# One written order for three schedulers: attention's end, token mixing and the MLP's first rounds of a fused layer

## The chip, the core and the metric

The kernel runs on one core of a Trainium2 chip. The metric is the device time of one execution in microseconds (us). The engines are called here as the profile calls them: PE (matrix products; PEld is its weight load), DVE (vector), ACT (scalar), POOL (GpSimd) and SP, which here only issues transfers. Each engine works through its own queue in order, and a wait at the head of a queue holds everything behind it.

## What is computed

The reference chains three blocks over x of shape 2 x 768 x 512 (two batches, 768 tokens, 512 channels):

```python
mask = q_bucket[:, :, :, None] == k_bucket[:, :, None, :]          # 6 hash bits for each token
scores = np.where(mask, 1 / np.sqrt(D) * q @ k.T, -1e9)            # 2 batches x 8 heads, 768 x 768, D = 64
x = softmax(scores) @ v                                            # heads side by side: 2 x 768 x 512
theta = x @ w_theta
y = w_tok_r @ (x * np.cos(theta)) + w_tok_i @ (x * np.sin(theta))  # mixes tokens: 768 x 768, for each batch
u = x + y
x = u + np.maximum(u @ w_ch, 0)
xn = (x - mean) / np.sqrt(var + 1e-6) * g_ln
out = x + np.maximum(xn @ w_ch1, 0) @ w_ch2                        # 512 -> 2048 -> 512
```

## The kernel before

Products run with 32-bit operands that are each split into a high and a low part; three products (high x high, high x low, low x high) stand for one. So nearly every operand costs an ACT copy that makes the high part and a subtraction that makes the low part, on DVE or on POOL. Weights arrive as 64-bit numbers and are rebuilt as 32-bit ones first: `conv_y` (ACT), `conv_s` (POOL, the `cs` tiles), `conv_bits` (two DVE instructions), then the high and the low part.

The work has four stages.

- **Attention**, 48 blocks of 256 query rows. One step of the loop touches several blocks at once: scores `s`, row maximum `m`, exponential `p`, normalised `pn` on POOL, three groups of four 128x128 transposes on PE (`U0` to `U2`, tile `t`), the high part on ACT (`H0` to `H2`, `pth`), the low part on DVE (`L0` to `L2`, `ptl`), the product with v (`PV`, tile `o`), and its eviction in two parts (`O` on ACT, `X` on DVE) into `XT`. The order of these steps is written by hand (`plan_s`, `plan`, `plan_b`) up to step 47. The last steps, which only finish blocks 45 to 47, were in the scheduler's hands.
- **Mixing.** For each batch b and each of six blocks j of 128 tokens, `mix_z` splits a block of x (`xh`, `xl`), transposes it on PE (`xps` or `xth`), copies that into `U` on ACT, makes 12 products of 512 columns with w_theta (tile `th` or `xth`), reduces the angle (DVE `t`, POOL `kk`, DVE `r`, DVE clamp of `r`), takes Abs and two Sin on ACT, multiplies by x on DVE, and splits both results (tile `z` or `arena`: high part ACT, low part DVE). These feed the token product `acc`: two halves of the output tokens, six blocks j, three groups t of 128 output tokens, two batches, six products of 512 columns each. The first half of the output was in the scheduler's order; the second half (`half1`) is an order written by hand in which one step (`mix.N`) holds both batches, 12 products. `mix_add` on DVE adds `acc` into `U`.
- **Channel product** with w_ch (12 chunks `ch_*`: transposes `ut`, split `uxh`/`uxl`, 12 products, DVE residual and statistics), layer normalisation (`ln_*`, `xn`), its transposes and sums (`xb_*`); these stand between the mixing steps and the MLP's first rounds, in the orders `half1` and `trans`.
- **MLP**, 16 rounds (`prod`, `snap`, `h_*`, `o_mm`, `o_add`). Rounds 0 to 2 stand in `trans`, the fourth and later ones in the repeated orders `odd` and `even`.

PSUM has few banks: in the mixing, the transposed block and the angle of one b share a bank (tags `T1`, `T2`), or two halves of one tile (`S0`, `S1`) for the first blocks.

Of the kernel before, what the change touches and what calls it, by code (L numbers as in the profile page):

```python
# [29 lines left out]
PI_LO = 3.1415925  # L30
# [3 lines left out]
def attn_moe_kernel(  # L34
# [80 lines left out]
    def conv_s(t, y, s):  # L115
        pool.tensor_scalar(out=s, in0=f(t)[:, :, 1], scalar1=0.0, scalar2=1.0, op0=ALU.mult, op1=ALU.mult)  # L116
# [553 lines left out]
    steps += [(k, plan_b if k - 2 in bq else plan) for k in range(4, NPER + last)]  # L670
    for k, now in steps:
        if k == NPER:
            order.close()
            bctx.close()
# [19 lines left out]

    up = ctx.enter_context(tc.tile_pool(name="u", bufs=1, reuse_waits="tile"))
# [7 lines left out]
    tok_t, tok_st = {}, {}  # L703

    def tok_load(half, j):
        tok_st[half, j] = [
            w_load(mp, w[j * 128:(j + 1) * 128, half * TW:(half + 1) * TW], bufs=4) for w in (wrT, wiT)
        ]

    def tok_conv(half, j):  # L710
        th, tl = (mp.tile([128, 2, TW], F32R, tag=x, bufs=2, name=f"{x}{half}{j}") for x in ("tokh", "tokl"))
        for x, t in enumerate(tok_st.pop((half, j))):
            w_conv(mp, t, th[:, x, :], tl[:, x, :])
        tok_t[half, j] = (th, tl)

    def ch_conv():
        WA["h"], WA["l"] = (
            const.tile([128, 4, 512], F32R, tag=f"X{x}", name=f"ch{x}") for x in range(2)
        )
        for c in range(4):  # L720
            for x in range(2):
                r = slice(256 * x, 256 * x + 256)
                w_conv(
                    mp, w_load(mp, w_ch[c * 128:(c + 1) * 128, r], "cst", 4), WA["h"][:, c, r], WA["l"][:, c, r], vec
                )

    def mix_banks(b, j):

        if j == 0:
            t = psum.tile([128, 2, 512], F32, tag=f"S{b}", name=f"xth{b}")  # L730
            return lambda x: t[:, x, :]
        return lambda x: bank(f"T{1 + b}", ("xps", "th")[x] + f"{b}{j}")

    z_s = {}
# [4 lines left out]
    def mix_z(b, j):  # L739
        c = b * NI + j  # L740
        if j == 0:
            z = mp.tile([128, 2, 2, 512], F32R, tag=f"z{b}0", name=f"z{b}0")
        else:
            z = arena[0][:, 2 * j - 2 + b, :].rearrange("p (y h n) -> p y h n", y=2, h=2)
        src = XT[b][:, :, j * 128:(j + 1) * 128]
        xh, xl = (up.tile([128, 512], F32R, tag=x, bufs=2, name=f"{x}{c}") for x in ("xh", "xl"))
        xh, xl = (x.rearrange("p (a s) -> p a s", a=4) for x in (xh, xl))
        cast(act, xh, src)
        sub(vec, xl, src, xh)
        banks = mix_banks(b, j)  # L750
        xps = banks(0)
        x = U[:, c, :]
        for d in range(4):
            pe.transpose(xps[:, d * 128:(d + 1) * 128], src[:, d, :], ident)
        act.activation(x, xps, AF.Copy)
        ps = banks(1)
        k = 0
        for d in range(4):
            for lt, w in ((xh, "h"), (xh, "l"), (xl, "h")):
                pe.matmul(ps, lt[:, d, :], WA[w][:, d, :], start=(k == 0), stop=(k == 11))  # L760
                k += 1
        t, kk, r = (tmp(y) for y in ("t", "kk", "r"))
# [12 lines left out]
        z_s[b, j] = z
# [3 lines left out]
    def mix_acc(half):  # L779
        for b in range(B):  # L780
            t = psum.tile([128, 2, 512], F32, tag=f"S{b}", name=f"acc{half}{b}")
            acc_t[half, b, 0], acc_t[half, b, 1] = t[:, 0, :], t[:, 1, :]
            acc_t[half, b, 2] = bank("T0" if b == 0 else "O", f"acc{half}{b}")

    def mix_mm(half, j, t):
        if j == 0 and t == 0:
            mix_acc(half)
        th, tl = tok_t[half, j]
        for b in range(B):
                acc, z = acc_t[half, b, t], z_s[b, j]  # L790
                k = 0
                for x in range(2):
# [7 lines left out]
    def mix_add(t, half=1):  # L800
        for b in range(B):
            u = U[:, b * NI + half * TH + t, :]
            vec.tensor_tensor(out=u, in0=acc_t[half, b, t], in1=u, op=ALU.add)
# [513 lines left out]
```

## Time and profile before

| | |
|---|---|
| median of three runs | 691.59 us (691.1 to 694.54) |
| the profiled execution's own time | 691.84 us |
| its span in the trace | 690.0 us, 11241 instructions |
| PE busy | 668.8 us, 97% of the span |
| DVE / ACT / POOL busy | 553.0 / 418.6 / 358.3 us |

The 1.84 us between span and time lie around the traced span. "Busy" of PE counts each product from its start to a modelled end, and products overlap, so an idle stretch of PE in the trace is a little shorter than the time that it costs.

### The profile page before, as it was taken

The page shows a single profiled execution, that of the slowest core. Times are in us where ns is not written, and L with a number is a line of the kernel's source. Part 1 is how long each engine was busy: PE and PEld are TensorE (multiplying, and loading weights), DVE is VectorE, ACT ScalarE, POOL GpSimd, SP SyncE. Part 2 cuts the span into 40 slices and gives each one's busy share as a digit, 9 for nine tenths or more (in the row PEclk, how much of TensorE's full clock was granted, in tenths as well). Part 3 has the DMA queues.
Part 4 walks back from the last instruction along what each step waited for, and adds up shares of the span by engine and source line. Part 5 has one row for each costly group of instructions (what it writes and reads, how often), then busy time and mean ns, then how long its engine had stood idle before and what let it go on. Part 6 is the DMA issues. An engine that isn't in the chain of part 4 may idle for free.

```text
span 690.0 us, 11241 instructions
## 1 busy us (share of the span) xinstructions
PE 668.8 (97%) x3790; PEld 593.1 (86%) x3790; DVE 553.0 (80%) x958; ACT 418.6 (61%) x864; POOL 358.3 (52%) x500
## 2 busy tenths in 40 slices
PE   9999999999999899999799989999999999999997
PEld 8899999999999777878578868889889898998986
DVE  5899988999999998897996376986666776767654
ACT  6799998999999866576442544463334434344321
POOL 5788998776776823334365975251523325050500
PEclk9999999999999999999999999999999999999999
DMA  8875654575550411112341301101121111111013
GB/s 250 208 156 154 156 113 110 126 161 126 136 153 18 138 46 47 47 46 62 129 119 58 123 1 61 62 1 34 62 90 62 61 62 62 61 62 62 0 47 137
DMA packets 32229, 62.23 MB, mean 90 GB/s; under 512 B 4466, under 2 KB 11460, under 8 KB 32173
## 3 DMA queue, kind: packets, MB, share of 16 engines
q1 hardware_dynamic: 32173, 61.53, 31.2%
q8 instruction: 30, 0.49, 0.3%
q14 instruction: 26, 0.21, 0.1%
HBM read 39.98 MB, written 3.15 MB: 62 GB/s over the span
## 4 chain that ended last, share of the span: by engine, by line
PE 83%; DVE 10%; issue 3%; ACT 3%; POOL 1%; DMA 0%; ACTq 0%; POOLq 0%; DVEq 0%
PE o L1110 19%; PE zy L1075 11%; PE acc L794 10%; PE o L391 9%; PE s L310 9%; PE t L366 9%; PE v L1075 5%; PE th L760 3%; PE a L843 3%; DVE cs L120 2%; PE bits L262 2%; DVE cy L123 1%; PE warm L473 1%; PE s L483 1%; DVE ptl L100 1%
## 5 line engine op out<-in xcount | busy, mean ns | idle before, releaser
L1110 PE MATMUL o<-arena,hh 128*128 128x512 f32 x384 | 119.4, 392 | 0.0
L353 POOL TENSOR_SCALAR pn<-p,l,m 128x768 f32<-128x768 f32 x96 | 95.8, 999 | 33.9 <-DVE l L349 23.6
L319 DVE TENSOR_REDUCE m<-s 128x1 f32<-128x772 f32 x96 | 91.1, 949 | 4.9 <-PE s L495 2.3
L100 DVE TENSOR_TENSOR ptl<-t,pth 128x512 fp32r<-128x512 f32 x144 | 90.6, 679 | 0.6 <-ACT pth L375 0.5
L335 ACT ACTIVATE p<-s,m 128x768 f32<-128x768 f32 x96 | 87.3, 910 | 2.7 <-DVE m L319 2.2
L375 ACT ACTIVATE pth<-t 128x512 fp32r<-128x512 f32 x144 | 81.5, 600 | 5.4 <-PE t L366 3.9
L310 PE MATMUL s<-tk,tq 128*128 128x386 f32 (+1 forms) x360 | 82.4, 350 | 0.2 <-ACT p L335 0.2
L366 PE MATMUL t<-ident,pn 128*128 128x128 f32 x576 | 81.2, 274 | 1.3 <-DVE ptl L100 0.7
L1117 DVE TENSOR_TENSOR U<-o,U 128x512 f32<-128x512 f32 x96 | 65.8, 686 | 19.4 <-PE o L1110 18.7
L1083 ACT ACTIVATE sn<-zy 128x384 f32<-128x384 f32 x48 | 23.6, 492 | 94.5 <-PE zy L1075 94.4
L116 POOL TENSOR_SCALAR cs<-st 128x512 f32<-128x512 f32 (+2 forms) x76 | 47.1, 628 | 64.9 <-DVE cy L123 61.3
L1110 PEld LDWEIGHTS o<-arena,hh 128*128 128x128 f32 x384 | 70.7, 188 | 9.8
L794 PE MATMUL acc<-arena,tokh 128*128 128x512 f32 x240 | 76.5, 395 | 1.5 <-DVE arena L100 1.0
L1110 PE MATMUL o<-arena,hl 128*128 128x512 f32 x192 | 76.1, 396 | 0.0
L366 PEld LDWEIGHTS t<-ident,pn 128*128 128x128 f32 x576 | 67.8, 141 | 9.5 <-POOL m L326 1.7
L310 PEld LDWEIGHTS s<-tk,tq 128*128 128x128 f32 (+1 forms) x360 | 59.3, 190 | 0.4 <-ACT p L335 0.4
L794 PEld LDWEIGHTS acc<-arena,tokh 128*128 128x128 f32 x240 | 44.3, 188 | 11.2 <-DVE arena L100 1.4
L120 DVE SCALAR_TENSOR_TENSOR cs<-st,cs 128x512 uint32<-128x512 uint32 (+2 forms) x76 | 47.5, 627 | 5.4 <-POOL cs L116 5.3
L1041 POOL TENSOR_TENSOR s<-cy 128x256 f32<-128x256 f32 x7 | 5.4, 776 | 88.7 <-DVE cy L123 88.7
L1100 DVE SCALAR_TENSOR_TENSOR hl<-c,hh 128x384 fp32r<-128x384 f32 x48 | 28.6, 598 | 27.6 <-ACT hh L1096 27.6
L123 DVE SCALAR_TENSOR_TENSOR cy<-cy,cs 128x512 uint32<-128x512 uint32 (+2 forms) x72 | 44.5, 623 | 6.8 <-ACT cy L113 2.7
L1096 ACT ACTIVATE hh<-c 128x384 fp32r<-128x384 f32 x48 | 25.1, 523 | 37.5 <-DVE c L1090 36.3
(216 smaller groups left out, 1561.5 us busy)
## 6 DMA issues: line engine op xcount, KB each, us to landing
st<-in_w_dram SPq DMA_DIRECT2D x36, 256.0 KB
st<-in_w_dram SPq DMA_DIRECT2D x14, 512.0 KB
tk<-hik SPq DMA_DIRECT2D x30, 193.0 KB
tq<-hiq SPq DMA_DIRECT2D x30, 192.0 KB
st<-in_wrT_dram SPq DMA_DIRECT2D x12, 384.0 KB
st<-in_wiT_dram SPq DMA_DIRECT2D x12, 384.0 KB
vs<-in_v_dram SPq DMA_DIRECT2D x8, 384.0 KB
out_dram<-U SPq DMA_DIRECT2D x12, 256.0 KB
```

The source lines that it names most:

```text
L100: eng.tensor_tensor(out=o, in0=i, in1=f(hi), op=ALU.subtract)
L310: pe.matmul(ps[:, hf, 0:HW], lt[0:K, x * 128:(x + 1) * 128], rt[0:K, hf, :], start=(K == 128), stop=(K != 128),)
L319: vec.tensor_reduce(out=m_t[p][:, 0, i:i + 1], in_=s_ps[p, i][:, :, 0:HW], axis=AX.XY, op=ALU.max, negate=True)
L335: act.activation(pt, ps[:, :, 0:HALF], AF.Exp, bias=m[:, 0, i:i + 1], accum_out=l_t[p][:, 0, i:i + 1])
L353: pool.tensor_scalar(out=pn.rearrange("p c s -> p (c s)"), in0=p_t.pop((p, i)).rearrange("p c s -> p (c s)"), scalar1=l_t[p][:, 1, i:i + 1 ...
L366: pe.transpose(ps[:, w * 128:(w + 1) * 128], pn_t[p, i][:, c, :], ident)
L375: act.activation(ph, t_ps[p, u], AF.Copy)
L391: pe.matmul(ps, vv[:, c, e].rearrange("p a d -> p (a d)"), x[:, c::NI, :], start=(k == 0), stop=(k == 2 * NI - 1),)
L794: pe.matmul(acc, w[:, x, t * 128:(t + 1) * 128], z[:, x, y, :], start=(j == 0 and k == 0), stop=(j == NI - 1 and k == 5),)
L1075: pe.matmul(ps_t[r, b], W1[g][y][:, w, d, :], XB[s][x][:, z, d, :], start=(first == 1 and k == 0), stop=(k == 5), skip_group_check=True,)
L1110: pe.matmul(ps, lt[:, i * 128:(i + 1) * 128], W2[g][:, y, x, :], start=(k == 0), stop=(k == 5))
L1117: vec.tensor_tensor(out=u, in0=o_t.pop((r, t)), in1=u, op=ALU.add)
```

## The change

Three things change, all between the attention's last steps and the end of the third MLP round.

1. The scheduler's two stretches are gone. A new written order `tail` holds the last attention steps (`U0.46` to `X.47`) together with the first two blocks of the mixing; `half1` is rewritten to hold the whole mixing, and `trans` is rewritten. `mix_z` is cut into fourteen small steps (`z_tab`, `z_h` ... `z_w`) so that an order can place each. `z_tab` is a new tiny Sin on ACT, which brings the Sin table in ahead of its first real use. The attention's `heads` pool is closed at the same point as before; `arena` is still made only after the attention's last product.
2. A mixing step now names its batch: `mix.N.b` is six products of one batch, with N from 0 to 35 over both halves; `madd` names half, group and batch.
3. The steps that make low parts, `conv_s`, the angle's `kk`, the clamp of `r`, the layer normalisation's `xn` and `w1_s` take a last number that chooses the engine: 0 is DVE, 1 is POOL. In the repeated rounds the numbers give the same engines as before.

PE has the same 3792 products and transposes, ACT one table step more (771 instructions instead of 770), DVE 980 instead of 960, POOL 485 instead of 505. By kind:

| instruction | on POOL before -> now | on DVE before -> now |
|---|---|---|
| clamp of `r`, 128x512 | 0 -> 11 | 12 -> 1 |
| `kk` of the angle, 128x512 | 12 -> 10 | 0 -> 2 |
| low part of the mixed blocks `z`/`arena`, 128x512 | 0 -> 8 | 24 -> 16 |
| low part of the token weights `tokl`, 128x384 | 24 -> 16 | 0 -> 8 |
| `cs` of the weights, 128x384 and 128x256 | 48 -> 40 | 0 -> 8 |
| low part of the MLP's input `xr` (to `arena` and `xb`), 128x384 | 16 -> 8 | 12 -> 20 |
| `xn`, 128x256 | 24 -> 16 | 0 -> 8 |

Five more low parts of weights, 256 or 512 columns wide, move from POOL to DVE.

```diff
-    for k, now in steps: ... if k == NPER: order.close(); bctx.close()
...
-        vec.tensor_scalar(out=r, in0=r, scalar1=PI_LO, scalar2=-PI_LO, op0=ALU.min, op1=ALU.max)
+    def z_tab():
+        act.activation(up.tile([128, 6], F32, tag="bns", bufs=2, name="tab")[:, 0:1], halfpi, AF.Sin)
+    def z_t(b, j):
+        if b + j < 2:
+            t = psum.tile([128, 2, 512], F32, tag=f"S{1 - j}", name=f"xth{b}{j}")
+            zb[b, j] = t[:, 0, :], t[:, 1, :]
+    def z_u(b, j):
+        act.activation(U[:, b * NI + j, :], zb[b, j][0], AF.Copy)
+    def z_c(b, j, e):
+        r = zr[b, j][0]
+        (vec, pool)[e].tensor_scalar(out=r, in0=r, scalar1=PI_LO, scalar2=-PI_LO, op0=ALU.min, op1=ALU.max)
+    def z_w(b, j, y, e):
+        sub((vec, pool)[e], z_o[b, j][:, y, 1, :], zr[b, j][1 + y], z_o[b, j][:, y, 0, :])
...
-    def mix_mm(half, j, t):
+    def mix_mm(half, j, t, b):
...
+        mix=lambda q, b: mix_mm(q // 18, q % 18 // TH, q % TH, b), madd=mix_add,
...
+    tail = """
+        U0.46 z_h.0.0 L2.45 nb.46 z_tab X.44 ld.t.0.0 z_l.0.0 U2.46 ld.t.0.1 R1.47 PV.45 H0.46 R2.47 nb.47
+        H2.46 L0.46 z_h.0.1 U1.46 na.47 L2.46 cv_y.t.0.0 z_t.0.0 H1.46 z_l.0.1 U2.47 z_u.0.0 cv_s.t.0.0.1 L1.46
...
-        mix.0 ch_ah.0 ld.t.2.0 ld.t.2.1 ch_al.0 cv_y.t.1.0 cv_s.t.1.0 cv_y.t.1.1 ch_at.1 cv_s.t.1.1
+        mix.2.0 z_r.1.0 z_q.0.1.1 z_p.0.1.0 z_h.1.2 z_w.0.1.1.0 z_t.0.2 z_q.0.1.0
+        mix.0.0 z_c.1.0.1 z_u.0.2 z_w.0.1.0.0 z_f.1.0.0 ld.t.2.0 z_l.1.2 z_m.0.2 z_f.1.0.1 ld.t.2.1 z_a.1.1
...
+    run(tail)
+    actx.close()
+    zq = zctx.enter_context(tc.tile_pool(name="z", bufs=1, side="right", reuse_waits="tile"))
+    arena.append(zq.tile([128, 2 * NI - 2, 2048], F32R, name="arena"))
```

What stands in the queues now, at three places. First ACT, from the eviction of attention block 44 (`ot`) on; `xT_75` is batch 0 of the attention's output, `xh` the high part of a mixing block, `pth` the high parts of attention blocks 46 and 47, `U` the copy of the transposed mixing block. Before:

```order
L400 ACTIVATE ot_3748<-o_3730 64x256
L113 ACTIVATE cy<-st 128x384
L755 ACTIVATE U<-xth_3872 128x512
L375 ACTIVATE pth_3760<-t_0_3752 128x512
L113 ACTIVATE cy<-st 128x384
```

Now:

```order
L400 ACTIVATE ot_3748<-o_3730 64x256
L93 ACTIVATE xh_3763<-xT_75 128x512
L709 ACT_TABLE_LOAD
L709 ACTIVATE tab<-halfpi 128x1
L375 ACTIVATE pth_3796<-t_0_3758 128x512
L375 ACTIVATE pth_3796<-t_2_3775 128x512
L93 ACTIVATE xh_3804<-xT_75 128x512
L113 ACTIVATE cy<-st 128x384
L375 ACTIVATE pth_3796<-t_1_3807 128x512
L731 ACTIVATE U<-xth_3817 128x512
```

The first `U` was second after `ot`; it is ninth now, behind the table load, three `pth` and two `xh`.

Second DVE, up to `xl` of the first block of batch 1 (`xT_76`), which that block's angle product reads. Before, from the third `cs` step on:

```order
L120 SCALAR_TENSOR_TENSOR cs<-st,cs 128x384 x2
L407 TENSOR_TENSOR xT_76<-o_3780,ot_3795 64x256
L123 SCALAR_TENSOR_TENSOR cy<-cy,cs 128x384
L100 TENSOR_TENSOR ptl_3806<-t_0_3797,pth_3805 128x512
L765 TENSOR_TENSOR r<-xth_3872,kk 128x512
L100 TENSOR_TENSOR ptl_3806<-t_1_3809,pth_3805 128x512
L123 SCALAR_TENSOR_TENSOR cy<-cy,cs 128x384
L120 SCALAR_TENSOR_TENSOR cs<-st,cs 128x384
L100 TENSOR_TENSOR ptl_3806<-t_2_3815,pth_3805 128x512
L766 TENSOR_SCALAR r<-r 128x512
L100 TENSOR_TENSOR xl_3908<-xT_76,xh_3907 128x512
```

Now, from the last `ptl` of block 47 on:

```order
L100 TENSOR_TENSOR ptl_3852<-t_0_3904,pth_3851 128x512
L407 TENSOR_TENSOR xT_76<-o_3882,ot_3911 64x256
L747 TENSOR_SCALAR t<-xth_3874 128x512
L120 SCALAR_TENSOR_TENSOR cs<-st,cs 128x384
L123 SCALAR_TENSOR_TENSOR cy<-cy,cs 128x384
L407 TENSOR_TENSOR xT_76<-o_3940,ot_3959 64x256
L777 TENSOR_TENSOR t<-t,U 128x512
L777 TENSOR_TENSOR kk<-kk,U 128x512
L757 TENSOR_TENSOR r<-xth_3874,kk 128x512
L100 TENSOR_TENSOR xl_3973<-xT_76,xh_3972 128x512
```

The clamp (L766) has left this queue, and `xl` of batch 1 now stands behind the eviction of attention's last block and the two products with `U`.

Third POOL, from its first work on the token weights on. Before:

```order
L116 TENSOR_SCALAR cs<-st 128x384 x2
L100 TENSOR_TENSOR tokl_3946<-cy,tokh_3945 128x384 x2
L764 TENSOR_SCALAR kk<-t 128x512
L116 TENSOR_SCALAR cs<-st 128x384 x2
L100 TENSOR_TENSOR tokl_4053<-cy,tokh_4052 128x384 x2
L116 TENSOR_SCALAR cs<-st 128x384
```

Now:

```order
L116 TENSOR_SCALAR cs<-st 128x384 x2
L100 TENSOR_TENSOR tokl_3862<-cy,tokh_3861 128x384
L116 TENSOR_SCALAR cs<-st 128x384
L752 TENSOR_SCALAR kk<-t 128x512
L100 TENSOR_TENSOR tokl_3862<-cy,tokh_3861 128x384
L762 TENSOR_SCALAR r<-r 128x512
L116 TENSOR_SCALAR cs<-st 128x384
L100 TENSOR_TENSOR tokl_3933<-cy,tokh_3932 128x384
L752 TENSOR_SCALAR kk<-t 128x512
L100 TENSOR_TENSOR tokl_3933<-cy,tokh_3932 128x384
L100 TENSOR_TENSOR z_3986<-t,z_3986 128x512
L762 TENSOR_SCALAR r<-r 128x512
```

The clamp `r` and a low part `z` of the mixed blocks now stand among the token weights' steps.

## Rows read from the trace of the kernel before

**Rows 1.** The page: busy time, share of the span and instructions of each engine.

```profile
PE 668.8 (97%) x3790; PEld 593.1 (86%) x3790; DVE 553.0 (80%) x958; ACT 418.6 (61%) x864; POOL 358.3 (52%) x500
```

**Rows 2.** Windows: stretch and length, each engine's busy us, granted clock, DMA share.

```profile
228.00:240.00 12.00, 9.91 (x69) 8.45 (x67) 11.35 (x21) 9.13 (x20) 10.90 (x13) 1.00 0.49 145
240.00:250.00 10.00, 8.65 (x35) 6.50 (x36) 9.81 (x15) 8.94 (x17) 4.79 (x6) 0.83 0.35 108
250.00:320.00 70.00, 68.37 (x320) 56.05 (x319) 61.61 (x98) 44.28 (x83) 23.55 (x26) 1.00 0.15 46
320.00:460.00 140.00, 130.57 (x630) 107.83 (x629) 105.92 (x206) 65.33 (x138) 80.43 (x98) 1.00 0.21 70
460.00:660.00 200.00, 200.00 (x1002) 179.93 (x1001) 138.46 (x231) 78.06 (x157) 64.66 (x75) 1.00 0.16 53
```

**Rows 3.** PE's waits, 228 to 460 us: waited for, total us, times, longest.

```profile
PE ut L828 <- DVE uxl L100: 4.8, 4, 2.1
PE ut L828 <- DVE U L803: 1.5, 1, 1.5
PE acc L794 <- DVE U L803: 1.5, 1, 1.5
PE xth L760 <- ACT U L755: 1.1, 2, 1.0
PE o L391 <- DVE xT L407: 1.1, 1, 1.1
PE acc L794 <- ACT z L93: 1.1, 1, 1.1
PE acc L794 <- DVE arena L100: 1.0, 1, 1.0
...
```

**Rows 4.** PE's timeline, 227 to 250 us: start, us, instruction, count.

```profile
227.86 0.60 PE L754 MATMUL xth<-ident,xT 128*128 128x128 f32 x4
...
233.40 0.88 PE L391 MATMUL o<-pth,vv 128*128 128x256 f32 x6
...
234.83 1.47 PE L366 MATMUL t<-ident,pn 128*128 128x128 f32 x12
...
244.63 0.63 PE L760 MATMUL xth<-thh,xh 128*128 128x512 f32 x1
245.06 0.63 PE L760 MATMUL xth<-thl,xh 128*128 128x512 f32 x1
...
247.41 0.39 PE L760 MATMUL th<-thh,xl 128*128 128x512 f32 x1
247.64 0.39 PE L760 MATMUL th<-thh,xh 128*128 128x512 f32 x1
```

**Rows 5.** ACT's timeline, 228 to 250 us.

```profile
229.01 0.38 ACT L400 ACTIVATE ot<-o 64x256 f32<-64x256 f32 x1
...
231.28 1.09 ACT L375 ACTIVATE pth<-t 128x512 fp32r<-128x512 f32 x2
...
243.32 1.28 ACT L769 ACT_TABLE_LOAD   x1
244.62 0.63 ACT L769 ACTIVATE kk<-r 128x512 f32<-128x512 f32 x1
```

**Rows 6.** DVE's and POOL's timeline, 241 to 251 us.

```profile
242.50 2.09 DVE L100 TENSOR_TENSOR xl<-xT,xh 128x512 fp32r<-128x512 f32 x2
241.29 2.15 POOL L100 TENSOR_TENSOR tokl<-cy,tokh 128x384 fp32r<-128x384 f32 x2
250.71 0.68 DVE L100 TENSOR_TENSOR xl<-xT,xh 128x512 fp32r<-128x512 f32 x1
```

**Rows 7.** Groups on POOL and DVE, 228 to 460 us: count, busy us, mean ns.

```profile
L764 POOL TENSOR_SCALAR kk<-t 128x512 f32<-128x512 f32 x12 | 10.4, 864 | 31.1 <-DVE t L763 19.0 <-ACT kk L769 5.0 <-ACT xh L93 4.7
L100 POOL TENSOR_TENSOR arena<-s,arena 128x512 fp32r<-128x512 f32 x2 | 2.5, 1298 | 0.0
L766 DVE TENSOR_SCALAR r<-r 128x512 f32<-128x512 f32 x12 | 7.2, 601 | 0.1
```

More of the change, by code (lines that the diff above doesn't have):

```diff
@@ L669, in attn_moe_kernel @@
     steps = [(k, plan_s) for k in range(4)] + [(4 - 1, plan)]
-    steps += [(k, plan_b if k - 2 in bq else plan) for k in range(4, NPER + last)]
+    steps += [(k, plan_b if k - 2 in bq else plan) for k in range(4, NPER)]
     for k, now in steps:
-        if k == NPER:
-            order.close()
-            bctx.close()
         late = now is plan and k < 4
@@ L701, in attn_moe_kernel @@
     TW = TH * 128
[L703 to L732, printed above, removed]
@@ L775, in mix_z, with z_a, z_k @@
-        z_s[b, j] = z
-    acc_t = {}
[L779 to L782, printed above, removed]
+        zr[b, j] = [ps]
+    def z_a(b, j):
+        t = tmp("t")
+        vec.tensor_scalar(out=t, in0=zr[b, j][0], scalar1=1.0 / TWO_PI, scalar2=MAGIC, op0=ALU.mult, op1=ALU.add)
+        zr[b, j].append(t)
+    def z_k(b, j, e):
+        kk = tmp("kk")
+        (vec, pool)[e].tensor_scalar(out=kk, in0=zr[b, j][1], scalar1=-MAGIC, scalar2=-TWO_PI, op0=ALU.add, op1=ALU.mult)
+        zr[b, j].append(kk)
@@ new lines, in attn_moe_kernel, with z_p, z_q @@
+    z_o = {}
+    def z_p(b, j, y):
+        s = zr[b, j][1 + y]
+        vec.tensor_tensor(out=s, in0=s, in1=U[:, b * NI + j, :], op=ALU.mult)
+    def z_q(b, j, y):
+        if (b, j) not in z_o:
+            z_o[b, j] = (
+                mp.tile([128, 2, 2, 512], F32R, tag=f"z{b}0", name=f"z{b}0") if j == 0
+                else arena[0][:, 2 * j - 2 + b, :].rearrange("p (y h n) -> p y h n", y=2, h=2)
+            )
+        cast(act, z_o[b, j][:, y, 0, :], zr[b, j][1 + y])
+    def z_w(b, j, y, e):
+        sub((vec, pool)[e], z_o[b, j][:, y, 1, :], zr[b, j][1 + y], z_o[b, j][:, y, 0, :])
@@ L788, in mix_mm @@
         th, tl = tok_t[half, j]
[L789 to L792, printed above, removed]
-                    for w, y in ((th, 0), (th, 1), (tl, 0)):
-                        pe.matmul(
-                            acc, w[:, x, t * 128:(t + 1) * 128], z[:, x, y, :],
-                            start=(j == 0 and k == 0), stop=(j == NI - 1 and k == 5),
-                        )
-                        k += 1
@@ L800, in mix_add @@
[L800 to L803, printed above, removed]
-    seq = [(half, j) for half in range(2) for j in range(NI)]
-    ORD = [b * NI + half * TH + t for half in range(2) for b in range(B) for t in range(TH)]
-    tok_load(0, 0)
-    mix_z(0, 0)
-    mix_z(1, 0)
-    tok_conv(0, 0)
-    tok_load(0, 1)
-    pad(up, 64, "pad2")
-    actx.close()
-    zq = zctx.enter_context(tc.tile_pool(name="z", bufs=1, side="right", reuse_waits="tile"))
@@ L815, in attn_moe_kernel, with mix_add @@
-    arena.append(zq.tile([128, 2 * NI - 2, 2048], F32R, name="arena"))
-    pad(zq, 56, "pad3")
+        acc, z = acc_t[half, b, t], z_o[b, j]
+        k = 0
+        for x in range(2):
+            for w, y in ((th, 0), (th, 1), (tl, 0)):
+                pe.matmul(
+                    acc, w[:, x, t * 128:(t + 1) * 128], z[:, x, y, :],
+                    start=(j == 0 and k == 0), stop=(j == NI - 1 and k == 5),
+                )
+                k += 1
+    def mix_add(half, t, b):
+        u = U[:, b * NI + half * TH + t, :]
+        vec.tensor_tensor(out=u, in0=acc_t[half, b, t], in1=u, op=ALU.add)
@@ L1008, in cv_to @@
         if kind == "t":
[L1009 to L1014 removed]
+            (half, j), x = divmod(r[0], NI), r[1]
+            if (half, j) not in tok_t:
+                tok_t[half, j] = tuple(
+                    mp.tile([128, 2, TW], F32R, tag=y, bufs=2, name=f"{y}{half}{j}") for y in ("tokh", "tokl")
+                )
+            return [y[:, x, :] for y in tok_t[half, j]]
+        if kind == "c":
+            return [WA[y][:, r[0], 256 * r[1]:256 * r[1] + 256] for y in "hl"]
         if kind == "e":
```

353 lines of the change are left out of this document (207 added, 146 removed).

## The prediction

> **What bounds the kernel now.** The page comes first: PE is busy 97% of the span and no other engine over 80% [rows 1]. So the change can win only time in which PE waits or runs slowly, and that has to be found by stretch. The windows show it [rows 2]: from 460 us on PE is busy 200.00 of 200.00 us, so the repeated MLP rounds have nothing to give, and they keep their order. From 228 to 460 us, the stretch that is written anew, PE is idle 2.09 + 1.35 + 1.63 + 9.43 = 14.5 us.
>
> PE's own waits say for whom [rows 3]: almost always for DVE (the low part `uxl`, the addition into `U`, the low part in `arena`), a little for ACT. DVE is not full there: over the 232 us it works 11.35 + 9.81 + 61.61 + 105.92 = 188.7 us, 81% [rows 2]. The waits are local: a queue in the wrong order, or a chain between two PE instructions that stand too near to each other.
>
> Idle time is less than what a wait costs, and the timeline gives the difference [rows 4]: a product of 512 columns lasts 0.39 us, but the next starts 0.23 us after it, so each wait costs 0.16 us more than its idle time; the eleven waits shown make 1.8 us. And in the window from 240 to 250 us the granted clock is 0.83, with starts 0.43 us apart where they are 0.23 us apart later [rows 2, 4]: the engine ran at the lower of its two levels (1.2 and 2.4 GHz) for about a third of that window, after it had waited several times in the 10 us before. 17% of the 8.65 us of work is 1.5 us. So what can be won at most is 14.5 + 1.8 + 1.5 = **17.8 us**.
>
> **The change, part by part.** PE's work is the same, instruction for instruction in kind, so the time changes by what is left of these 17.8 us. I follow the new queues from 227.86 us, where PE meets its first changed instruction [rows 4].
>
> *The tail, first wait.* PE now has four transposes five times and one product with v ahead of the first angle product. Twelve transposes take about 1.3 us, 0.11 each, so 5 x 0.44 = 2.2 us, and a product with v 234.83 - 233.40 = 1.43 us [rows 4]: PE arrives at 231.5 us. That product waits for the copy `U` of the same tile; such waits are in the trace [rows 3]. On ACT, `U` now stands ninth behind `ot`. `ot` ended at 229.39; copies follow each other in about 0.5 us (two in 1.09); the table load took 1.28 [rows 5]. Seven copies, the load and the tiny Sin (0.2, an estimate from the small end of these rows) make 5.0 us, less 0.5 because one `xh` that stood ahead of `ot` has left its place: `U` ends at 233.9. **PE waits 2.4 us.** Before, the load stood at 243.32, in the first block's own chain; it had to be paid once either way.
>
> The Trainium skill ("ScalarE: Activation LUTs", What ACT_TABLE_LOAD costs) puts the load with its drain at about 2.66 us, which would make this wait 1.4 us longer and the time 684.7. The trace does not agree: the load begins at 243.32 and the next Sin at 244.62, 1.30 us in all [rows 5]. The sum goes by the row.
>
> *The tail, second wait.* From 233.9 PE makes the first angle product (12 x 0.23), eight transposes, a product with v, four transposes, the second angle product, the last product with v and eight transposes: 2 x 2.76 + 2 x 1.43 + 20 x 0.11 = 10.6, so 244.5 us. The third matrix product then needs `xl` of batch 1. In DVE's queue `xl` stands behind the eviction of attention's last block, which can start only once the last product with v (ended about 243.7) has been copied by ACT (0.38, [rows 5]): 244.1. Then `xT`, about as short as that copy, and four of 0.68 [rows 6]: two products with `U`, `r` and `xl`; 247.2. PE can do two of its products meanwhile, so the wait is about 2.2 us if these run alone, and 3.7 if each is held as `xl` was at 242.50, where two took 2.09 us beside POOL's `tokl`, instead of 0.68 each [rows 6]. I take 2.6. The tail keeps **5.0 us**; the bounds are 2 (both overlap) and 9 (ACT and DVE both late by 2 more).
>
> *The clock.* Two waits of over 2 us stand near each other, as several did before the low clock at 242. Whether the clock falls again the order cannot tell; I put half of the 1.5 us: **0.8**, bounds 0 and 3 (twice).
>
> *Work that changes its engine.* Off DVE go eleven clamps at 0.60 [rows 7] and eight low parts at 0.68 [rows 6]: 12 us. On to it come sixteen low parts of 384 columns and 23 instructions mostly shorter, at 0.4 to 0.55 (0.68 scaled by their columns, an estimate): about 19. DVE ends near 196 us of a stretch of some 223, 88%. POOL gets clamps (its `kk`, the nearest row, 0.86) and low parts (1.30) [rows 7], 20 us, and loses 39 instructions, at 0.86 some 33. On POOL the clamp alone is 0.26 us slower and the low part 0.62, which lengthens each chain by about 0.9 us; in the new order a chain has 9 to 23 us of other PE work (counted in the order, 0.23 for a product) between its angle product and its first mixing product, against about 7.5 us of its own instructions at the durations of [rows 5 to 7]. I cost this at nothing; if that cover is gone, 12 blocks x 0.9 = 11 us come back. SP issues the same transfers; the loads of w_ch, half of which stood ahead of the third token block's, now follow the seventh's. None of the waits shown is for a transfer, and the DMA share is at most 0.49 [rows 2]; this too costs nothing, or, if a block came late, a wait at its first product.
>
> *The rest, 250 us on.* Before, 11.1 of the idle us lie here. The w_ch conversions, which stood in one lump just ahead of the channel product, are now spread over fourteen half steps; the additions into `U` are made per batch, so that the second half's first product no longer waits for the last of the first. What stays? The best measure is the row from 250 to 320 us: DVE busy 61.61 of 70, also 88%, and PE idle 1.63, 2.3% [rows 2]. Over the 210 us left that is 4.8 us. One of those waits, 1.1 us on `z` [rows 3], falls at a first mixing product, where the new order leaves over 9 us; without it **3.7 us**. Bounds: 1 and 11.1 (as before).
>
> **The sum.** 5.0 + 0.8 + 3.7 = 9.5 us stay of 17.8; 8.3 are won. The profiled execution took 691.84 us; 691.84 - 8.3 = 683.5. It stands 0.25 above the median of the runs, 691.59, so the prediction is **683.3 us**.
>
> **Rivals.**
>
> 1. *DVE and POOL hold each other.* For: at 242.50 each `xl` took 1.04 us beside POOL, while POOL's `tokl` took 1.07 [rows 6]; and POOL's work in the tail grows denser. Some 17 instructions on DVE before the first mixing product read SBUF alone; at 0.4 us more each, with two thirds of them beside POOL, that is 4.5 us: 687.8. Against: over the whole stretch POOL has 13 us less to do. The Trainium skill states this as a rule: the two share one pair of SBUF ports as an exclusive lock ("SBUF — State Buffer", its section on the two sides), and moving work between them might not help ("Perfetto Trace Analysis", Optimizing Scalar/DVE Operations). By that rule the trace agrees at 242.50, not where DVE reads PSUM.
> 2. *The waits only move.* Each wait that the order removes comes back one PE instruction later, because the chain behind it is as long as ever. For: PE's idle time before was in a hand-made order too, 9.43 us from 320 on [rows 2]. Against: DVE's idle share there is a quarter, so room exists. Time: 691.6, within 0.5%.
> 3. *Slower: the split by batch.* One step with two batches gave a late block 2.76 us of cover; now a half step has 1.38. If a half step waits 0.3 us on average, 72 of them make 21.6 us, more than everything that can be won: 695.4. It decides from 0.25 us per half step on. Against: from 250 to 320 us the waits make 1.6 us over 36 half steps, 0.05 each.
>
> **How the numbers follow.** My forecast gets 0.68 (677.5 to 688: the bounds of the tail, clock and rest taken together, not all at one end), the first rival 0.14, the second 0.11, the third 0.07. The range from 677.5 to 689 holds the forecast nearly whole and most of the first rival, and leaves the second and third out, about 2 in 10. About 0.5% (3.5 us) is what a measurement of this kernel tells from no change: faster is below 688.1. That is nearly all of the forecast and 0.12 of rival one: 0.80; within it 0.13; slower 0.07.
>
> **What would show it.** In the changed kernel's profile: PE idle between 228 and 250 us about 5 us, with the first wait on ACT's `U` near 232 and the second on DVE's `xl` near 245; PE idle from there to the fourth MLP round under 5 us, no wait over 1.5; the clock row below 1.00 in at most one window of 10 us; the repeated rounds the same, only earlier. The clamp on POOL should last 0.7 to 1.0 us. I am wrong if PE's idle time in the tail is over 9 us, if mixing products show many waits of 0.2 to 0.4 us for `z` or `arena`, or if POOL's low parts end last there.

## The result and the profile after

The changed kernel takes 684.22 us, the median of four runs (683.67 to 686.27); four runs of the kernel before, taken with it, have a median of 693.07. The ratio is 0.988 (95% interval 0.984 to 0.992): 1.2% less, in an interval that leaves out 1. The prediction was 683.3, with a range from 677.5 to 689.0. The profiled execution took 684.06 us with a span of 682.3, against 690.0 before.

The page of the changed kernel, with busy time, share of the span and number of instructions for each engine, beside [rows 1]:

```profile
PE 667.8 (98%) x3790; PEld 593.6 (87%) x3790; DVE 564.1 (83%) x978; ACT 419.4 (61%) x865; POOL 348.5 (51%) x480
```

The windows of the changed kernel, to be laid beside [rows 2] (columns as there):

```profile
228.00:240.00 12.00, 10.13 (x67) 8.79 (x68) 10.33 (x18) 9.88 (x20) 7.58 (x10) 1.00 0.21 67
240.00:250.00 10.00, 6.96 (x35) 5.24 (x34) 9.55 (x14) 6.92 (x14) 7.54 (x7) 0.86 0.27 79
250.00:260.00 10.00, 10.00 (x38) 7.99 (x38) 6.59 (x10) 5.73 (x11) 1.99 (x3) 0.79 0.00 0
250.00:320.00 70.00, 69.14 (x312) 56.65 (x312) 61.59 (x83) 45.67 (x84) 39.33 (x38) 0.97 0.20 61
320.00:460.00 140.00, 138.43 (x676) 116.35 (x675) 123.79 (x256) 69.09 (x147) 58.44 (x70) 1.00 0.23 76
```

PE is idle 1.87 + 3.04 + 0.86 + 1.57 = 7.3 us between 228 and 460 us, where it was idle 14.5. But the two parts go opposite ways. From 250 us on, 11.1 idle us became 2.4. In the tail, from 228 to 250, 3.4 became 4.9, and the granted clock is now low in two windows, 0.86 and 0.79, where before it was low in one. A low clock shows as full busy time: PE is busy 10.00 of 10.00 us from 250 to 260, and yet it issues only 38 products and transposes there (46 in experiment 1 below, at full clock).

PE's waits from 226 to 460 us in the changed kernel (us in total, times, longest), beside [rows 3]; two smaller groups are left out:

```profile
PE xth L741 <- ACT U L731: 2.4, 2, 2.0
PE xth L741 <- DVE xl L100: 0.9, 1, 0.9
PE t L366 <- POOL cs L116: 0.9, 1, 0.9
PE ut L834 <- DVE uxl L100: 0.9, 2, 0.5
PE xps L728 <- DVE r L757: 0.9, 1, 0.9
PE t L366 <- DVE ptl L100: 0.6, 1, 0.6
```

The waits for `mix_add`, the additions into `U`, are gone, and that for `uxl` fell from 4.8 to 0.9. The largest wait left is one of 2.0 us in the tail, for ACT. PE's timeline there (start, duration, what, idle time before it and its releaser):

```profile
246.88 0.50 PE L741 MATMUL xth<-thh,xh 128*128 128x512 f32 x1 [2.04 <-ACT U L731]
247.21 0.55 PE L741 MATMUL xth<-thl,xh 128*128 128x512 f32 x1
248.70 0.80 PE L741 MATMUL xth<-thh,xl 128*128 128x512 f32 x1 [0.94 <-DVE xl L100]
249.29 0.63 PE L741 MATMUL xth<-thh,xh 128*128 128x512 f32 x1
249.72 0.63 PE L741 MATMUL xth<-thl,xh 128*128 128x512 f32 x1
...
254.29 0.40 PE L741 MATMUL th<-thh,xh 128*128 128x512 f32 x1
254.52 0.40 PE L741 MATMUL th<-thl,xh 128*128 128x512 f32 x1
```

After the two waits the starts are 0.43 us apart until 254, and 0.23 apart from then on, the two distances of [rows 4]. What held `U` back is seen in ACT's timeline:

```profile
245.57 0.63 ACT L93 ACTIVATE z<-t 128x512 fp32r<-128x512 f32 x1 [0.18 <-DVE t L777]
246.22 0.60 ACT L731 ACTIVATE U<-xth 128x512 f32<-128x512 f32 x1
```

It stands behind the high part `z<-t` of another block, and that waited for DVE's product `t*U`. DVE's timeline has this product, and `xl` behind two more instructions:

```profile
244.85 0.69 DVE L777 TENSOR_TENSOR t<-t,U 128x512 f32<-128x512 f32 x1
245.46 1.48 DVE L777 TENSOR_TENSOR kk<-kk,U 128x512 f32<-128x512 f32 x1
246.86 0.68 DVE L757 TENSOR_TENSOR r<-xth,kk 128x512 f32<-128x512 f32 x1
247.47 2.19 DVE L100 TENSOR_TENSOR xl<-xT,xh 128x512 fp32r<-128x512 f32 x2
```

Two of these rows are longer than such instructions are alone; POOL's timeline shows what ran beside them:

```profile
244.96 1.44 POOL L100 TENSOR_TENSOR tokl<-cy,tokh 128x384 fp32r<-128x384 f32 x1 [1.05 <-ACT tokh L93]
246.35 1.74 POOL L100 TENSOR_TENSOR z<-t,z 128x512 fp32r<-128x512 f32 x1
```

So part of each wait comes from a queue in which the awaited instruction stands behind work that could have waited. Another part is the stretch beside POOL: alone, `kk*U` would have been 0.8 us shorter and the first `xl` 0.4 to 0.5.

One wait of the list has the wrong name. The profile puts the 0.9 us at 232.26 down to POOL's `cs`, but the transposes there (block 47, third group) read no `cs`. What they need is their bank, and the last to read it is DVE's second `ptl` of block 46, which ends at 232.11:

```profile
232.26 0.63 PE L366 MATMUL t<-ident,pn 128*128 128x128 f32 x4 [0.93 <-POOL cs L116]
230.82 1.29 DVE L100 TENSOR_TENSOR ptl<-t,pth 128x512 fp32r<-128x512 f32 x2 [1.37 <-ACT pth L375]
230.19 1.08 ACT L375 ACTIVATE pth<-t 128x512 fp32r<-128x512 f32 x2
```

Those `ptl` waited 1.37 us for ACT's `pth`, which stand right behind the table load (228.67 to 229.95) and the tiny Sin.

### The profile page after: what moved, and what is told of

Read it like the earlier page. It is cut to its first block, busy times and chain, and to the rows that moved or that the text cites. A ratio compares the mean times of both kernels' runs of the same rounds, so it can differ in the third digit from the quotient of the medians.

```text
span 682.3 us, 11230 instructions
## 1 busy us (share of the span) xinstructions
PE 667.8 (98%) x3790; PEld 593.6 (87%) x3790; DVE 564.1 (83%) x978; ACT 419.4 (61%) x865; POOL 348.5 (51%) x480
## 5 line engine op out<-in xcount | busy, mean ns | idle before, releaser
L116 POOL TENSOR_SCALAR cs<-st 128x512 f32<-128x512 f32 (+2 forms) x68 | 44.8, 666 | 71.8 <-DVE cy L123 53.5
L807 PE MATMUL acc<-arena,tokh 128*128 128x512 f32 x240 | 75.1, 394 | 0.1
L807 PE MATMUL acc<-arena,tokl 128*128 128x512 f32 x120 | 46.9, 390 | 0.0
```

What stands on the lines that cost most here:

```text
L807: pe.matmul(acc, w[:, x, t * 128:(t + 1) * 128], z[:, x, y, :], start=(j == 0 and k == 0), stop=(j == NI - 1 and k == 5),)
```

## Experiments

Executions of one kernel differ by about 2 us in the first 50 us, long before anything changed: in seven of the fourteen traces the granted clock of these 50 us is 0.97 and PE has begun 280 to 288 instructions by their end, in the other seven it is 1.00 and PE has begun 299 to 304. So medians are compared, and places in a trace are read from 228 us on. The kernel before has medians from 692.1 to 694.0 us in the sets of runs taken with the experiments, so a difference of under 2 us between medians of two sets tells little by itself. "This" is the median of its runs; ratios are to the kernel before on the same chip.

**1. The tail's second wait.** The base is the changed kernel; only the start of `half1` is put in another order.

```diff
-z_p.0.0.0 z_h.1.0 z_t.1.0 z_p.0.0.1 z_t.1.1 z_q.0.0.0 cv_l.t.1.1.1 z_r.0.1 z_u.1.0 z_h.1.1 z_l.1.0
-z_q.0.0.1 z_w.0.0.0.1 z_u.1.1 z_m.1.0 z_l.1.1 z_w.0.0.1.0 z_c.0.1.1 z_m.1.1 ...
+z_h.1.0 z_t.1.0 z_p.0.0.0 z_t.1.1 z_u.1.0 z_l.1.0 z_h.1.1 z_q.0.0.0 cv_l.t.1.1.1 z_r.0.1 z_p.0.0.1 z_u.1.1
+z_m.1.0 z_l.1.1 z_q.0.0.1 z_w.0.0.0.1 z_w.0.0.1.0 z_c.0.1.1 z_m.1.1 ...
```

> The order around attention's last block is changed again, nothing else: on ACT the copy U of batch 1's first tile goes ahead of the high part of z, on DVE the low part xl of batch 1 ahead of the second product with U. Theory (the second wait is a queue in the wrong order): PE's two waits there, 2.04 us for ACT's U and 0.94 us for DVE's xl, shrink to under 0.6 us together, and the low clock behind them goes with them; 680 to 682 us. Rival (the chain to the first mixing product is as long as ever, so the wait only moves): PE waits 2 to 3 us later, at the first mixing product for z, and the time stays 683.5 to 684.9 us.

This took 680.59 us (680.49 to 680.89), ratio 0.982 (0.979 to 0.985): 3.6 us less than the changed kernel. The windows of this kernel:

```profile
240.00:250.00 10.00, 8.50 (x46) 6.57 (x44) 9.54 (x13) 7.26 (x15) 7.46 (x8) 1.00 0.29 79
250.00:260.00 10.00, 9.99 (x46) 7.98 (x45) 10.00 (x15) 8.28 (x16) 4.54 (x6) 1.00 0.01 2
```

PE's timeline at the two waits:

```profile
246.38 0.50 PE L741 MATMUL xth<-thh,xh 128*128 128x512 f32 x1 [1.22 <-ACT U L731]
...
247.32 0.50 PE L741 MATMUL xth<-thh,xl 128*128 128x512 f32 x1 [0.22 <-DVE xl L100]
```

The two waits were 2.98 us together and are 1.44, more than the 0.6 expected; but the clock stays at 1.00 in both windows, and that is the larger part of the gain (an estimate: 2.6 us by the distances of the starts, against 1.5 for the shorter waits). So half of the second wait was queue order, and its price was the wait and the clock behind it.

**2. The old second half behind the new first half.** Tokens of `half1` from the first step of the second half on, and `trans`, in the order and shares of before; both batches of a step together.

```diff
-mix.18.1 cv_b.c.1.1 cv_l.c.1.0.0 ...
-mix.18.0 cv_y.c.2.0 cv_l.c.1.1.0 ...
+cv_b.c.1.1 cv_l.c.1.0.0 ... cv_l.c.3.1.0 ch_at.0
+mix.18.0 mix.18.1 ch_ah.0 ch_al.0 ...
```

> The order of before for the second half of the token mixing and the change to the MLP (both batches of a mixing step together, old shares of DVE and GpSimd there, w_ch's conversions in one lump ahead of it), behind the new tail and the new first half. Theory (what the change won lies in the rewritten second half and the change to the MLP): PE's losses from 320 us on come back, some 9 us, so 691 to 694 us. Rival (the new first half and the earlier conversions of w_ch made the room, and the order behind it is free): 683.5 to 687 us, with PE's idle time from 320 to 460 us under 5 us.

This took 698.12 us (696.94 to 699.14), ratio 1.007 (1.004 to 1.010). The loss is larger than forecast: the kernel is 14 us slower than the changed one and slower than before. Its waits of PE from 320 to 460 us:

```profile
PE ut L834 <- DVE uxl L100: 9.7, 3, 6.8
PE ut L834 <- DVE U L815: 1.5, 1, 1.5
```

So the second half is where the time lies, and one wait, behind w_ch's conversions, holds half of it. It is no price of the old second half, though: in the kernel before, the longest wait for `uxl` is 2.1 us [rows 3], and here 6.8. Experiments 6, 7, 10 and 12 take it apart.

**3. The shares alone.** The new order, each token with the engine that it had before.

```diff
-z_w.0.0.0.1 ... z_c.0.1.1 ... cv_l.t.2.0.0
+z_w.0.0.0.0 ... z_c.0.1.0 ... cv_l.t.2.0.1
```

> The new order with the old shares: clamps and low parts of z on DVE, kk on GpSimd, low parts of the token blocks on GpSimd, and so on, token for token in the new places. Theory (the shares cost and win nothing, the cover of 9 us and more in front of each first mixing product hides either): 683.2 to 685.2 us. Rival (the new order needs them: DVE is too full or GpSimd too late in the old shares): waits of PE for DVE or GpSimd of 3 us and more between 255 and 450 us, 687 to 691 us.

This took 684.83 us (683.76 to 688.32), ratio 0.989 (0.986 to 0.992), an interval that covers the changed kernel's. The shares neither won nor cost anything that can be measured.

**4. Both batches together, from the second token block on.** Each pair stands at the later of its two places. In this order one transposition for the channel product reads its tile before the last addition into it, so the result is not the layer's; the amount of work is the same.

```diff
-mix.5.1 z_a.0.3 z_u.1.3 ...
-mix.5.0 z_f.1.2.1 ...
-mix.8.0 z_w.1.2.1.0 ...
+mix.5.1 z_a.0.3 z_u.1.3 ...
+mix.5.0 z_f.1.2.1 ...
+z_w.1.2.1.0 ...
```

> Both batches of each mixing step run together again, from the second token block of the first half to the end of the second half, at the later of the two places; the rest of the order and the shares stay. Theory (splitting by batch costs nothing by itself and gives each block's chain more cover): some of the waits for z and for U at the steps' starts return, 685 to 688 us. First rival (the split is what won the 9 us): 690 to 694 us. Second rival (each half step pays for the split): faster than the changed kernel, under 683 us.

This took 697.76 us (694.65 to 701.42), ratio 1.008 (1.005 to 1.011). It decides little: the largest wait, 4.9 us for DVE's `r`, is at a transposition that stood between two half steps and now comes ahead of both. The joining moved PE's other work too, so this is not the price of the split. Experiment 7 is made to avoid that.

**5. The table load out of the way.** Experiment 1 with one token moved.

```diff
-U0.46 z_h.0.0 L2.45 nb.46 z_tab X.44 ... cv_h.t.0.0 cv_b.t.0.1
+U0.46 z_h.0.0 L2.45 nb.46 X.44 ... cv_h.t.0.0 z_tab cv_b.t.0.1
```

> The mended order of the first experiment, with one more move: the tiny Sin that carries the table load leaves its place between two copies that PE waits for, and goes on ACT behind the first tokh, where ACT was idle for 1.83 us. Theory (the first wait of the tail is ACT's queue with the load in it): PE starts its first angle product 0.6 to 1.2 us earlier; 679.2 to 680.1 us. Rival (the chain over the softmax's last normalisations on GpSimd ends last there, and ACT's queue does not count): 680.4 to 680.9 us, as without the move.

This took 680.78 us (679.97 to 682.14), ratio 0.982 (0.980 to 0.984), as experiment 1. The 0.9 us that the profile puts down to POOL's `cs` went, and the first angle product starts 4.87 us after the tail's first transposes, where it was 6.06 in the changed kernel. That is the start 1.2 us earlier that the theory forecast, and the chain on GpSimd that the rival named did not hold PE there. But a new wait came at the next product with v, and took the time back:

```profile
PE o L391 <- DVE xT L407: 1.1, 1, 1.1
```

The load in ACT's queue held PE, but it was not all that bounded the tail; taking it out moved the wait to the bank that DVE's eviction frees.

**6. w_ch's conversions in one lump.** The changed kernel with all eight units behind the last step of the first half.

```diff
+mix.17.1 cv_y.c.0.0 cv_s.c.0.0.1 cv_b.c.0.0 cv_h.c.0.0 cv_l.c.0.0.0 ... cv_l.c.3.1.0 madd.0.2.0
 mix.18.1 madd.0.2.1
```

> The changed kernel with the conversions of w_ch put back into one lump, between the last mixing step of the first half and the first of the second; batches stay split, shares stay. Theory (the lump on DVE stood in front of the additions and low parts that PE needs for the channel product): a wait of PE for DVE's uxl of 4 to 7 us between 335 and 350 us, and 688 to 692 us. Rival (DVE catches up under the half steps' cover): all waits there under 2 us, 684 to 686 us.

This took 694.31 us (692.21 to 696.1), ratio 1.001 (0.999 to 1.003): the whole gain is gone. The wait is one of 9.4 us, but not at the expected place: PE's first product of the second half waits for DVE's addition into `U`, which frees its accumulator. The wait is not the whole price: the granted clock is 0.50 from 345 to 350 us, where PE takes up work again, and 0.68 from 350 to 355.

**7. Batches together in the second half alone.** Every z is long ready there; the places of the steps in the queue stay, but the order of the half steps in them is 18.0, 18.1, 19.0 and so on, and the additions follow the last product of their tile. The half steps stay half steps, with other engines' work between them as before.

```diff
-mix.18.1 ... mix.18.0 ... mix.19.1 ... mix.20.0 ... mix.33.1 ... mix.34.0 ... mix.35.1 ... mix.34.1 ... mix.35.0
+mix.18.0 ... mix.18.1 ... mix.19.0 ... mix.19.1 ... mix.33.1 ... mix.34.0 ... mix.34.1 ... mix.35.0 ... mix.35.1
```

> The changed kernel with the two batches of each mixing step side by side again in the second half alone, where every z is ready long before: the half steps fill the same places of the queue in the old order, and the additions follow the last product of their tile. Theory (a half step costs nothing by itself, and its cover matters only where z is made): 684 to 686.5 us, what comes back being the wait behind the last additions. First rival (the split itself is what won): 689 us and more. Second rival (each half step costs 0.1 us and more): under 682.5 us.

This took 687.7 us (684.88 to 689.35), ratio 0.991 (0.988 to 0.994): 3.5 us more than the changed kernel, past the theory's upper end. Its waits of PE from 320 to 460 us:

```profile
PE ut L834 <- DVE uxl L100: 2.9, 3, 1.5
PE ut L834 <- DVE U L815: 0.9, 1, 0.9
```

What comes back are the waits at the end of the half, where the transposition for the channel product needs the last additions, as the theory said, and larger than it said. The forecast of the second rival, under 682.5, did not come. But this order has as many half steps as the other, so it does not measure what a half step costs; the list of waits of the changed kernel does, and none in it is at a mixing product.

**8. Both waits of the tail.** Experiment 5, with `z_u.0.0` and `R2.47` earlier, and `z_h`, `z_l`, `z_t` and `z_u` of 1.0 ahead of `X.47`.

```diff
+... R2.47 z_l.0.0 ... z_t.0.0 z_u.0.0 H1.46 ... cv_y.t.1.1 z_h.1.0 ... z_t.1.0 PV.47 ... z_a.0.1 z_l.1.0 z_f.0.0.2 z_u.1.0 ... X.47
```

> The mended order with both waits of the tail taken up: the table load late as in the other kernel, U of the first block and the softmax's reciprocal one place earlier, and xh, xl, the transposition and U of batch 1's first block ahead of attention's last block, on whose output they do not depend. Theory (every wait of the tail is queue order): PE starts its first angle product near 232.0 and its third near 244.7 us, its losses in the tail fall by 3 to 4 us; 676.5 to 678 us. Rival (the chain to the first mixing product bounds the tail): PE waits instead at its first mixing products for z, 1.5 us and more, and the time is 679 to 680.6 us.

This took 679.17 us (678.72 to 681.15), ratio 0.980 (0.978 to 0.983): past the theory's upper end and just inside the rival's range, 679 to 680.6. The rival's place is wrong, since no wait is at a mixing product. The wait put down to POOL is gone and the two for ACT's `U` are 0.3 each, but two others stand in for them:

```profile
PE o L391 <- DVE xT L407: 1.2, 1, 1.2
PE th L741 <- DVE xl L100: 1.1, 1, 1.1
```

**9. Those two as well.** `X.45` ahead of the conversions on DVE, the z products and `xl` of 1.1 ahead of `X.47`, the first z's two low parts exchanged between the engines, and a few more tokens shifted with them.

```diff
+... L2.47 X.45 cv_h.t.0.0 z_tab z_a.0.0 cv_b.t.0.1 ... z_p.0.0.1 ... z_p.0.0.0 ... cv_b.t.1.1 z_h.1.1 ... z_l.1.1 ... X.47
```

> The tail's order mended once more, by what the last run left: the eviction of the block before last goes ahead of the conversions on DVE, so that the next product with v finds its bank free; the z products and xl of batch 1's first two blocks go ahead of attention's last eviction; the two low parts of the first z change engines. Theory (queue order, all of it): PE's remaining waits there, 1.21 us for DVE's xT and 1.10 us for DVE's xl, go, no wait over 0.6 us is left between 228 and 260 us, and the first mixing product starts near 249 us; 676 to 677.5 us. Rival (DVE and GpSimd are full there, each move makes something else late): a wait of 1 us and more at another place of the tail, 678.3 to 679.8 us.

This took 679.01 us (678.85 to 681.14), ratio 0.981 (0.978 to 0.983): no faster than experiment 8. The rival held. The new places are 0.8 us and 1.0 us for ACT's `U`:

```profile
PE th L741 <- ACT U L731: 1.1, 2, 1.0
PE xth L741 <- ACT U L731: 1.1, 2, 0.8
```

Experiments 1, 8 and 9 in turn brought 3.6, 1.4 and 0.2 us, the last two less than medians of two sets can tell, and each moved a wait. Whether the engines or my orders set that limit is not settled. Experiments 8 and 9, equal by their intervals, are the fastest versions found, and beat both kernels.

**10. The lump over four half steps.** Two units behind each, in front of the additions.

```diff
+mix.16.1 cv_y.c.1.0 cv_s.c.1.0.1 cv_b.c.1.0 cv_h.c.1.0 cv_l.c.1.0.0 ... cv_l.c.1.1.0 ld.c.3.1 madd.0.0.1
+mix.17.0 cv_y.c.2.0 ... cv_l.c.2.1.0 madd.0.1.1
```

> The changed kernel with w_ch's conversions two and two behind four half steps at the end of the first half, where the lump of the second experiment on it stood behind one and the change spreads them over fourteen. Theory (what costs is DVE work standing in one piece in front of what PE needs): between the two, 686 to 690 us, with waits of 1 to 3 us between 325 and 350 us. Rival (any place ahead of the channel product does, only the full lump is too late): 683.5 to 685.5 us.

This took 693.98 us (690.55 to 695.84), ratio 1.000 (0.998 to 1.003): both forecasts are wrong. DVE's timeline says why:

```profile
335.11 0.42 DVE L120 SCALAR_TENSOR_TENSOR cs<-st,cs 128x256 uint32<-128x256 uint32 x1
335.63 0.42 DVE L123 SCALAR_TENSOR_TENSOR cy<-cy,cs 128x256 uint32<-128x256 uint32 x1
336.54 0.43 DVE L100 TENSOR_TENSOR ch<-cy,ch 128x256 fp32r<-128x256 f32 x1 [0.48 <-ACT ch L93]
...
338.65 0.68 DVE L815 TENSOR_TENSOR U<-acc,U 128x512 f32<-128x512 f32 x1
...
342.80 0.68 DVE L815 TENSOR_TENSOR U<-acc,U 128x512 f32<-128x512 f32 x1
```

A unit takes 1.78 us of DVE's queue, 0.48 of it idle for ACT's copy, where a half step of PE lasts 1.38; and the additions stand behind such units. The one at 342.80 frees the accumulator:

```profile
343.63 1.19 PE L807 MATMUL acc<-z,tokh 128*128 128x512 f32 x2 [7.94 <-DVE U L815]
```

This is PE's one large wait there. Against experiment 6 the place where the lump begins changed little; what counts is how much stands ahead of the additions.

**11. The tail left to the scheduler.** The changed kernel, with the text `tail` ordered by the scheduler that ordered it before.

```diff
+order.close()
 run(tail)
+order.enter_context(tc.manual_schedule())
```

> The changed kernel with the tail alone, from attention's last blocks to its last eviction, left to the scheduler that ordered it before; all that follows keeps the order written by hand. Theory (the hand-made tail is no better than the scheduler's): 682.5 to 684.5 us. Rival (the hand-made tail did win, and the losses seen there stand in for larger ones): 685.5 to 690 us.

This took 687.72 us (686.96 to 689.31), ratio 0.993 (0.991 to 0.995): 3.5 us slower than the hand-made tail. Its tail has waits of 3.7 us for ACT's `U` and 2.8 us for the exponential `p`. So with this text the hand-made order does win. The text is not that of before, though, which made block 0 of both batches first; how the old tail would do in front of the new halves was not tried.

**12. Additions first, units in pairs.** The places of experiment 10, in two ways that the kernel before had: each addition goes ahead of the conversions, and the two units of a row run in pairs.

```diff
-mix.16.1 cv_y.c.1.0 cv_s.c.1.0.1 cv_b.c.1.0 cv_h.c.1.0 cv_l.c.1.0.0 ... cv_l.c.1.1.0 ld.c.3.1 madd.0.0.1
+mix.16.1 madd.0.0.1 cv_y.c.1.0 cv_y.c.1.1 ... cv_b.c.1.0 cv_b.c.1.1 cv_h.c.1.0 cv_h.c.1.1 cv_l.c.1.0.0 cv_l.c.1.1.0 ...
```

> The conversions of w_ch over the same four half steps as in the last experiment on them, in the two ways in which the kernel before had them: each addition into U goes ahead of the conversions that follow its product, and the two units of a row run in pairs, so that DVE does not stand idle (0.48 us a unit) between a unit's bits and its low part. Theory (the 8.1 us wait was the DVE work queued ahead of the additions that free the accumulators, 8 units of 1.78 us with the idle time): two pairs of about 2.7 us are left ahead of the last addition that the next half's first product needs, the wait shrinks to 2.5 to 4 us, and the time is 686.5 to 689.5 us. Rival (a lump at that place costs 8 to 9 us however it is ordered): 692 to 695 us.

This took 687.63 us (686.09 to 689.5), ratio 0.991 (0.989 to 0.994), inside the theory's range. PE's wait in this kernel:

```profile
PE acc L807 <- DVE U L815: 2.9, 1, 2.9
```

The windows around it:

```profile
330.00:340.00 10.00, 7.05 (x25) 5.41 (x25) 8.85 (x22) 4.96 (x13) 3.40 (x7) 0.83 0.74 230
340.00:350.00 10.00, 10.00 (x52) 8.24 (x51) 6.38 (x12) 4.80 (x10) 3.54 (x5) 1.00 0.39 113
```

The lump's price is DVE's queue ahead of the additions that free the accumulators: 7.9 us of wait in one order, 2.9 in the other, with the same instructions in the same four half steps. Two things changed at once here, the additions' places and the pairs; what each brought was not tried alone.

## Why the prediction was right, step by step

The total was right, and its terms were not all so: that it came out within 1 us is in part luck, since the clock was 2.3 us dearer than forecast, the rest 1.3 cheaper, and the tail's sum right with other parts. By the prediction's own count the changed kernel keeps 4.9 (tail) + 2.4 (rest) + 3.1 (clock) = 10.4 us where 5.0 + 3.7 + 0.8 = 9.5 were forecast; 17.8 - 10.4 = 7.4 us won, against a span 7.7 us shorter. Of these 7.7, PE gained 0.66 before it met its first changed instruction (at 227.20, before at 227.86), which no part of the change explains. The count itself is uneven: its ceiling has the 0.16 us by which a wait costs more than its idle time, for the eleven waits shown, and what stays has it for none. Counted alike on both sides (idle time, 0.16 us for each of the 17 and 10 waits that the full lists have, and the clock by the distances of the starts), 14.5 + 2.7 + 1.3 became 7.3 + 1.6 + 2.6: 7.0 us won, which is 7.7 - 0.66.

- **The ceiling** of 17.8 us from 228 to 460 us held: the repeated MLP rounds are as before (PE busy 199.87 of 200 us from 460 on).
- **The tail's first wait**, 2.4 us near 232 for ACT's `U`: in size near, in cause half right. It came in three pieces, 0.57 for `ptl` at 228.40, 0.93 at 232.26 and 0.37 for `U` at 233.26. The load in ACT's queue, on which the sum rested, did hold PE, but mostly in the second piece, through `pth` and `ptl`, and not through `U`. Experiment 5 shows that it was not the only bound: without the load the product started 1.2 us earlier, and the next wait took that back. From the load's start to the next instruction there were 1.29 us again (228.67 to 229.96), as the row had it.
- **The tail's second wait**, 2.6 us for DVE's `xl`: measured 2.04 + 0.94. I followed DVE's queue and missed ACT's, on which `U` stands behind a copy that itself waits for DVE. Experiment 1 shows that half of this was order. The wait for `xl` goes with the stretch beside POOL, which the prediction had priced: run alone, `kk*U`, `r` and `xl` would have ended at about 247.4 (an estimate from 0.69 and 0.68 us each), before PE asked for `xl` at 247.76.
- **The clock** is the term that was mis-sized: 0.8 us forecast with bounds of 0 and 3, and 0.14 x 6.96 + 0.21 x 10.00 = 3.1 measured in the same way. By the starts it is 2.6: thirteen products took 5.6 us (248.70 to 254.29) where 0.23 apart they take 3.0. It fell for two windows where at most one was expected. Tail and clock together cost 3 us more than before, so the tail as it was written took from the gain.
- **Engine moves cost nothing**: right (experiment 3). The clamp on POOL lasts 0.95 us, in the expected 0.7 to 1.0. The cover of 9 us and more in front of the mixing products fits this, as none of the waits left is at one for `z` or `arena`; no run took the cover away.
- **The rest**, 3.7 us: 2.4 measured, none over 1.5. The sum was better in its reasons than in its working: it took the wait of 1.1 us off after the row had been scaled from 70 to 210 us, and taken off before, the row gives 1.6. The reasons given hold, though the conversions lie over twelve half steps and not fourteen. The spread of w_ch's conversions and the early additions are worth 3.4 us against the order of experiment 12, and 9.8 against that of experiment 10. The order of the half steps in the second half, with the additions by batch at its end, is worth 3.5 (experiment 7). How these add up to the gain, together with the tail's loss, was not measured in one kernel.
- **Rival 1** (DVE and POOL hold each other) is half true. The mechanism shows in the tail: DVE's `kk*U` took 1.48 us and ended 0.54 us after POOL's `tokl` did, where such a product takes 0.69 alone. The Trainium skill calls the shared port pair an exclusive lock ("SBUF — State Buffer", SBUF: two separate sides); by that rule the trace agrees here: most of the DVE instruction's work falls behind the end of POOL's. Over the twelve blocks the median of `kk*U` rose from 0.69 to 0.92 us. But the 4.5 us of this rival did not come: among PE's waits, the 0.94 us for `xl` is the one that can be traced to it here.
- **Rival 2** (the waits only move) fell for the kernel as a whole, and is true of the tail: experiments 5, 8 and 9 moved waits from one place to the next, at 1 us each.
- **Rival 3** (the split costs) fell: none of the waits left in the changed kernel is at a mixing product, and from 260 to 320 us experiment 8 has PE busy for all of the time, in half steps. What whole steps would cost was not measured cleanly: experiment 4 moved other work with them, and experiment 7 only changes the order of half steps.

```profile
260.00:320.00 60.00, 60.00 (x278) 49.13 (x276) 55.70 (x77) 39.93 (x73) 37.80 (x36) 1.00 0.23 71
```

## What to carry to other kernels

Before an accumulator or a bank is used again, count what stands ahead of the instruction that frees it on its engine, idle time for other engines included: that sum, less PE's other work, is the wait. In experiment 10 DVE turned to the first unit at 331.56 and had freed the accumulator at 343.48, 11.9 us; PE had other work for 4.1 of them, and waited 7.9. Follow every engine's queue to the awaited instruction, and look for one in it that waits itself; a copy behind a waiting copy cost more here than a slow one. A wait of 2 to 3 us on PE is to be priced with the low clock that can follow it, so that shortening it may pay twice.

## What the runs showed of the hardware

- The clock's price can exceed the wait's. Waits of 2.04 and 0.94 us within 2 us were followed by some 5 us at half speed (2.6 us lost, by the starts); the same two waits (2.04 and 1.0 to 1.1) in experiments 2, 4, 6, 7, 10 and 12 were followed by losses from 1.5 to 2.9; waits of 1.22 and 0.22 at the same place (experiment 1) by none. One of 2.9 us (experiment 12) took the clock to 0.83 in its window. Yet a wait of 2.1 us for `uxl` in the kernel before [rows 3] left the window from 320 to 460 us at 1.00 [rows 2].
- DVE instructions with two operands in SBUF are stretched beside POOL, in the changed kernel to as much as 2.6 times their time: `kk*U` to 1.50 instead of 0.69, `xl` to 1.77 instead of 0.68. Where no wait of PE hung on it, that cost nothing: in experiment 8 PE is busy for all of 260 to 320 us, while the median `kk*U` took 0.87.
- The first 50 us of an execution vary by about 2 us, with the clock at 0.97 or 1.00: the first transposes of the mixing blocks, with the same work ahead of them, begin near 231 us in experiments 1, 7, 8 and 12, and 233.1 to 233.8 in 2, 3, 4, 6 and 10. It sets how small a difference single traces can show.
